# Values over 96 partitions with sums moved by small transfers, flat keys for the second batch, and another order up to the 4th chunk

## The chip, the cores and the metric

The kernel runs on one core of a Trainium2 chip. The time is that of one execution on the device in microseconds; it is taken three times, and the median counts. Besides, one execution was recorded by the profiler, and the rows below come from it.

## The reference

Pooled attention is followed by a gated product. Batch and heads are 8 and 8, the sequence is 576 and a head 64 wide; keys and values are averaged over groups of 8 positions, which leaves 72 keys for each head. The weights come as float64.

```
k_p = k.reshape(B, H, Sp, 8, D).mean(axis=3);  v_p = the same of v        # Sp = 72
attn = softmax(q @ k_p^T / sqrt(D));  x = (attn @ v_p) as (4608, 512)
a = x @ w1;  b = x @ w2                                                  # 512 x 1024 each
out = ((a * b) @ w3) @ w_out                                             # w3 1024 x 1024, w_out 1024 x 512
```

## The kernel before

The product `w3 @ w_out` is formed once on the chip (`W`, 8 tiles), so that a token chunk needs `x @ w1`, `x @ w2`, their product and one product with `W`. Each of these is made of three passes over a high and a low part of both factors (`PASSES`). The 4608 tokens are 12 chunks `m` of 384.

**The start** turns float64 into float32 by bit operations: a load brings 512 KB of raw words (`load_wo`, `load_w3`, `load_w12`), `w_high` takes the upper word on ScalarE (L140), `w_low` the rest of the fraction on VectorE (L145) or ScalarE (L150), `w_or` joins them on VectorE (L154). Tiles of `w3` are transposed by TensorE (`w_turn`, L183) and split (`t_hi`, `t_lo`), those of `w_out` split alone (`o_hi`, `o_lo`), and `w_mm s it` (L613, three passes of 128x512) adds them into `W`; there are 16 `s` with 4 `it` each. The same is done to the tiles of w1 and w2 (`w12_high`, `w12_low`, `w12_or`, `w12_hi`, `w12_lo`).

**A chunk** is, for each of 8 `j`: `a_mm` and `b_mm` (12 matmuls each, L538), `g_mul`, `g_hi`, `g_lo` and `out_mm` (9 matmuls, L582), which adds into three banks. The attention of chunk n + 1 lies between the matmuls of chunk n: `s_mm` (L415, scores), `soft_max` to `soft2`, a turn of the weights (`pt_mm` with `pt_post`, L475 and L485, in the first two chunks; `pt_turn` on VectorE and `pt_move` by DMA, L491 and L498, after them), `av_mm` (L512, 32 rows of keys at a time), and `x_hi`, `x_lo`.

**Keys and values** of a batch come in tiles of 2 x 8 x 64 floats a partition (`load_k`, `load_v`, four buffers `st`), and a tree of three additions on GpSimd (`pool_tree`, L373, L374, L378) sums the groups of 8. For the values each of three steps `r` reads 32 keys a head that overlap with the next step's, in four transfers of 32 partitions, and the sums are written into `vm` where `av_mm` reads them. Keys of a batch in `FLAT` come row by row over 128 partitions (three loads, the last a small one); of the others a load brings two heads over 72 partitions (four loads). `kt_mm` (L350) transposes the sums, and `kt_post` scales them into `kbd`.

**The order** of all steps is written out in `ORDER` up to some place in chunk 3; what isn't in it follows by the numbers of `at(...)`. Every engine takes its own instructions in that order, one after another, and waits for what it needs; a transfer that must wait on SyncE (SP) holds up all transfers behind it, and at most 8 transfers are on their way. Tables say which engine takes a step that two could take (`LOW_ACT`, `LOW_DVE`, `LO_DVE`, `O_POOL`, `K_DVE`, `Q_DVE`, `PT_DVE`, `A_DVE`). The cells of the raw words of w1 and w2 are those that earlier weight tiles leave: `load_w12 0 0` takes the cell of the first w_out tile, free after `w_mm 8` has run for all four `it`, `load_w12 7 1` that of `w_mm 15`.

Of the kernel before, what the change touches and what calls it, by code (L numbers as in the profile page):

```python
# [19 lines left out]
def kernel(  # L20
# [766 lines left out]
    for b in range(1, B):  # L787
# [13 lines left out]
        load_w3 2; w_high w3 2; w_or wo 0; o_hi 0; w_low w3 2; load_wo 2; w_or w3 2; w_turn 2; t_hi 0;
        w_mm 0 0 (0,); t_lo 0; w_mm 0 2 (0,); w_mm 0 3 (0,); warm 4; o_lo 0; w_mm 0 2 (1,); w_mm 0 0 (1,);
        w_mm 0 1 (0,); w_high wo 2; w_low wo 2; load_w3 1; w_mm 0 3 (1,); w_high w3 1; w_low w3 1;
        w_mm 0 3 (2,); load_w3 3; w_or w3 1; w_turn 1; w_mm 0 1 (2,); w_or wo 2; t_hi 2; w_mm 0 2 (2,); t_lo 2;
        o_hi 2; o_lo 2; w_mm 2 3 (0,1,2); load_wo 1; load_wo 3; w_high wo 1; w_low wo 1; w_or wo 1;
        w_mm 2 0 (0,1,2); load_w3 6; w_high w3 3; t_hi 1; w_low w3 3; o_hi 1; w_mm 2 2 (0,1,2); w_mm 1 3 (0,);
        w_low wo 3; t_lo 1; w_mm 0 1 (1,); w_mm 1 1 (0,); load_wo 4; w_high wo 3; load_w3 4; w_mm 1 1 (2,);
        o_lo 1; w_mm 1 2 (1,); load_w3 5; w_mm 1 3 (2,); w_mm 0 0 (2,); w_high w3 6; load_w3 7; load_wo 5;
# [145 lines left out]
```

## Time and profile before

| | us |
|---|---|
| median of three runs (lowest, highest) | 737.97 (737.64, 738.20) |
| the profiled execution | 739.05 |
| its span, first to last instruction | 737.2 |
| TensorE busy within the span | 722.3 |
| VectorE, ScalarE, GpSimd busy | 402.4, 228.6, 158.2 |

The profiled execution's own time is 1.85 us more than its span. TensorE is busy for 98% of the span; a matmul that waits at half speed counts as busy too, so that the idle time is read beside the granted clock.

### The profile page before, as it was taken

To read this page: it belongs to the slowest core of one execution; us is meant where nothing else is said; L and a number is where in the kernel's file an instruction comes from. 1 tells how busy PE (TensorE), PEld (TensorE's weight loads), DVE (VectorE), ACT (ScalarE), POOL (GpSimd) and SP (SyncE) were. 2 spreads that over 40 slices of the span, in tenths; PEclk is the share of its full clock that TensorE was granted. 3 is DMA by queue.
4 is the path that set the end of the run, shared out by engine and by line. 5 is a ranking of instruction groups with operands and counts; after the bars stand their busy time and mean duration, and the time that the engine had idled before them with its cause. 6 is when DMAs were issued, how large, how long until landed. Compare 5 with 4: busy or idle time off the path is not lost.

```text
span 737.2 us, 13685 instructions
## 1 busy us (share of the span) xinstructions
PE 722.3 (98%) x5466; PEld 652.9 (89%) x5466; DVE 402.4 (55%) x785; ACT 228.6 (31%) x506; POOL 158.2 (21%) x176
## 2 busy tenths in 40 slices
PE   6998999999999999999999999999999999999997
PEld 4876899998998999998998999998998999998997
DVE  6887976663653653743753742843743743732211
ACT  6886664222222222222222222222212222222211
POOL 1443438403305000025045100034054000000000
PEclk9999999999999999999999999999999999999999
DMA  9989962337240121153255130253345230210101
GB/s 332 354 263 242 239 175 60 57 97 157 59 131 12 61 68 25 64 125 85 78 131 123 65 79 9 73 129 72 101 116 114 82 70 2 82 27 1 43 1 44
DMA packets 124495, 74.57 MB, mean 101 GB/s; under 512 B 76176, under 2 KB 108176, under 8 KB 124432
## 3 DMA queue, kind: packets, MB, share of 16 engines
q1 hardware_dynamic: 124288, 73.57, 37.7%
q8 instruction: 43, 0.70, 0.4%
q14 instruction: 20, 0.16, 0.1%
q10 hardware_dynamic: 144, 0.13, 0.1%
HBM read 52.43 MB, written 9.44 MB: 84 GB/s over the span
## 4 chain that ended last, share of the span: by engine, by line
PE 92%; DMA 5%; SPq 1%; DVE 1%; issue 1%; POOL 0%; ACT 0%; DVEq 0%; POOLq 0%
PE o L582 26%; PE a L538 26%; PE b L538 26%; PE o L613 4%; PE a L512 3%; DMA raw<-in_moe_w_dram 2%; PE att L415 2%; DMA st<-in_k_dram 1%; PE att L183 1%; DMA PT<-T 1%; PE a L415 1%; PE a L613 1%; SPq L498 1%; PE att L512 1%; PE b L613 0%
## 5 line engine op out<-in xcount | busy, mean ns | idle before, releaser
L538 PE MATMUL a<-xT,hl 128*128 128x384 f32 x1152 | 217.5, 336 | 0.0
L538 PE MATMUL b<-xT,hl 128*128 128x384 f32 x1152 | 216.6, 335 | 0.0
L538 PEld LDWEIGHTS a<-xT,hl 128*128 128x128 f32 x1152 | 203.5, 188 | 6.9
L538 PEld LDWEIGHTS b<-xT,hl 128*128 128x128 f32 x1152 | 200.6, 188 | 1.1 <-issue 0.3
L582 PE MATMUL o<-Wc,gh 128*128 128x512 f32 (+1 forms) x576 | 180.4, 394 | 0.0
L556 DVE TENSOR_TENSOR a<-b,a 128x384 f32<-128x384 f32 x96 | 52.9, 552 | 196.3 <-PE b L538 190.5
L373 POOL TENSOR_TENSOR st<-st 128x512 f32<-128x512 f32 (+1 forms) x51 | 68.2, 1338 | 354.8 <-DMA st<-in_k_dram 262.7
L582 PEld LDWEIGHTS o<-Wc,gh 128*128 128x128 f32 x576 | 105.8, 189 | 23.0 <-issue 5.0
L582 PE MATMUL o<-Wc,gl 128*128 128x512 f32 (+1 forms) x288 | 113.2, 393 | 0.0
L561 ACT CAST gh<-a 128x384 fp32r<-128x384 f32 x96 | 49.3, 513 | 193.6 <-DVE a L556 181.8
L548 ACT COPY a<-a 128x384 f32<-128x384 f32 x92 | 44.1, 480 | 179.6 <-PE a L538 158.2
L567 DVE TENSOR_TENSOR gl<-a,gh 128x384 fp32r<-128x384 f32 x96 | 57.0, 595 | 29.2 <-ACT gh L561 29.2
L582 PEld LDWEIGHTS o<-Wc,gl 128*128 128x128 f32 x288 | 54.1, 188 | 12.2
L440 ACT ACTIVATE EB<-EB 128x288 f32<-128x288 f32 x66 | 29.4, 445 | 79.7 <-DVE EB L432 79.7
L491 DVE STREAM_TRANSPOSE T<-EB 128x768 f32<-128x768 f32 x30 | 46.8, 1561 | 10.9 <-DMA PT<-T 10.6
L452 DVE TENSOR_REDUCE sm<-EB 128x4 f32<-128x288 f32 x66 | 29.6, 450 | 25.8 <-ACT EB L440 25.8
L613 PE MATMUL o<-hl 128*128 128x512 f32 x144 | 40.3, 410 | 0.0
L374 POOL TENSOR_TENSOR st<-st 128x256 f32<-128x256 f32 (+1 forms) x51 | 38.9, 764 | 4.0
L613 PEld LDWEIGHTS o<-hl 128*128 128x128 f32 x144 | 26.6, 193 | 5.3 <-DVE Wc L624 0.2
L512 PE MATMUL a<-PT,vm 32*64 32x384 f32 (+1 forms) x192 | 28.1, 417 | 2.4 <-ACT PT L485 1.7
L459 DVE TENSOR_TENSOR EB<-EB,sm 128x576 f32<-128x576 f32 x36 | 28.3, 786 | 1.3
L512 PE MATMUL att<-PT,vm 32*64 32x384 f32 (+1 forms) x576 | 28.6, 419 | 0.3 <-DVE qT L301 0.3
(89 smaller groups left out, 560.3 us busy)
## 6 DMA issues: line engine op xcount, KB each, us to landing
raw<-in_moe_w_dram SPq DMA_DIRECT2D x32, 512.0 KB
st<-in_v_dram SPq DMA_DIRECT2D x96, 128.0 KB
PT<-T SPq DMA_DIRECT2D x120, 96.0 KB
out_dram<-ob SPq DMA_DIRECT2D x35, 256.0 KB
st<-in_k_dram SPq DMA_DIRECT2D x28, 288.0 KB
qs<-in_q_dram SPq DMA_DIRECT2D x112, 48.0 KB
raw<-in_moe_w_out_dram SPq DMA_DIRECT2D x8, 512.0 KB
qs<-in_q_dram SPq DMA_DIRECT2D x96, 24.0 KB
```

The source lines that it names most:

```text
L373: nc.gpsimd.tensor_tensor(out=t[:, :, 0:4], in0=t[:, :, 0:4], in1=t[:, :, 4:8], op=ALU.add)
L374: nc.gpsimd.tensor_tensor(out=t[:, :, 0:2], in0=t[:, :, 0:2], in1=t[:, :, 2:4], op=ALU.add)
L452: nc.vector.tensor_reduce(out=Mt[n, t][1][:, hs], in_=parts(Et[n, t])[:, hs], axis=AX.XY, op=ALU.add)
L491: nc.vector.transpose(out=T.rearrange("p g u i -> p u g i"), in_=Et[n, t][:, :NU * P].rearrange("p (u j g) -> p u g j", u=NU, g=4))
L512: nc.tensor.matmul(out=ps[g][D * c:D * c + D, off:off + cnt], lhsT=vm[b % 2][rows, r, c], rhs=PT[n][rows, cc, 2 * r + c], start=(r == 0), ...
L538: nc.tensor.matmul(out=o, lhsT=w12[j, w][sw][:, kt * P:(kt + 1) * P], rhs=x[sx][:, kt], start=(i == 0), stop=(i == 3 * NK - 1))
L548: (nc.vector.tensor_copy if (m, j) in A_DVE else nc.scalar.copy)(out=a, in_=stage.pop(("a", m, j))[:, :CH])
L556: nc.vector.tensor_tensor(out=g, in0=ps[:, :CH], in1=g, op=ALU.mult)
L561: nc.scalar.copy(out=gh, in_=g)
L567: nc.vector.tensor_tensor(out=gl, in0=g, in1=f(gh), op=ALU.subtract)
L582: nc.tensor.matmul(out=oacc[m][t][x][:, cols], lhsT=(gh, gl)[sg][:, c], rhs=W[j][sw][:, cols], start=(j == 0 and i == 0), stop=(j == NJ - ...
L613: nc.tensor.matmul(out=wacc[h][it], lhsT=w3t[s][sa][:, it * P:(it + 1) * P], rhs=wo[j][sb], start=n == 1, stop=n == 3 * NJ)
```

## The change

Four things change. Values: a step `r` now holds the keys 3k + r, so that its 24 keys a head don't overlap; one transfer brings them over 96 partitions (4 heads x 24 keys, twice), the tree writes the sums into a new tile `vp`, and `move_v` copies them into `vm` by 8 transfers of 24 partitions a batch, issued by SyncE. The scores' keys are put in the same order by `kt_post`, which reads with a step of three. Second: `FLAT` has batch 1 as well. Third: the tables name other engines. Fourth: `ORDER` is another one, up to the same stretch, and `out_mm` may come in any order of `j`.

```diff
-    EW = 2 * P + 4
+    EW = 2 * P
-    LO_DVE = [(1, 1), (3, 0), (3, 1), (5, 1), (6, 1)]
-    FLAT = (0,)
+    LO_DVE = [(1, 0), (3, 0), (4, 1), (5, 0), (7, 1)]
+    FLAT = (0, 1)
-    LOW_ACT = [6 of w3, 3 of wo]
+    LOW_ACT = [8 of w3, 7 of wo]
-    O_POOL = [0, 3, 4, 6]
+    O_POOL = [2, 4]
-    K_DVE = [(0, 2), (1, 0), (1, 2), (1, 3)]
+    K_DVE = [(1, 3)]
...
+        nc.gpsimd.memset(vm[i], 0.0)
...
     def load_v(b, r):
         t = stage["v", b, r] = st_tile([P, 2, POOL, D])
-        keys = v[b, :, KG * r * POOL:(KG * r + 32) * POOL].rearrange("(g c) (k e) d -> g k c (e d)", c=2, e=POOL)
-        for g in range(4):
-            nc.sync.dma_start(out=t[32 * g:32 * g + 32].rearrange("p c e d -> p c (e d)"), in_=keys[g])
+        rows = v[b].rearrange("h (k r e) d -> r (h k) (e d)", r=KS, e=POOL)[r]
+        nc.sync.dma_start(
+            out=t[:VP].rearrange("p s e d -> p s (e d)"), in_=rows.rearrange("(s p) x -> p s x", p=VP))
...
     def prep_v(b, r):
-        pool_tree(stage.pop(("v", b, r)), vm[b % 2][:, r])
+        if b not in vp:
+            vp[b] = p1.tile([P, 2, KS, D], F32, tag="vp", name="vp")
+        pool_tree(stage.pop(("v", b, r))[:VP], vp[b][:VP, :, r])
+
+    def move_v(b, s):
+        for i in range(4):
+            g, c = divmod(4 * s + i, 2)
+            nc.sync.dma_start(out=vm[b % 2][32 * g:32 * g + KW, c], in_=vp[b][KW * i:KW * i + KW, s])
...
     def out_mm(m, j):
-        if j == 0:
+        if m not in oacc:
...
+        for s in range(2):
+            at("L", prep[-1] + 2, move_v, b, s)
...
     ORDER = """
-        load_wo 0; w_high wo 0; warm 5; w_low wo 0; load_w3 0; w_high w3 0; w_low w3 0; w_or w3 0; w_turn 0;
+        warm 5; load_w3 0; w_low w3 0; w_high w3 0; load_wo 2; w_high wo 2; w_or w3 0; warm 3; warm 4; w_turn 0;
```

The first place is SyncE's queue at the program's start (`raw` from `moe_w` is a tile of w3, from `moe_w_out` one of w_out). Before:

```order
L120 DMA raw<-in_moe_w_out_dram 128x1024
L125 DMA raw<-in_moe_w_dram 128x4x256 x2
L120 DMA raw<-in_moe_w_out_dram 128x1024
L125 DMA raw<-in_moe_w_dram 128x4x256 x2
L120 DMA raw<-in_moe_w_out_dram 128x1024 x2
```

And in the change:

```order
L126 DMA raw<-in_moe_w_dram 128x4x256
L121 DMA raw<-in_moe_w_out_dram 128x1024 x2
L126 DMA raw<-in_moe_w_dram 128x4x256
L121 DMA raw<-in_moe_w_out_dram 128x1024
L126 DMA raw<-in_moe_w_dram 128x4x256 x2
```

The tile of the second `w_turn` (`load_w3 2`) was the third transfer and is the fourth now; that of the first `w_turn` was the second and is the first.

The second place is SyncE's queue from the transfers behind the last w3 tile to the last keys of batch 1 (`raw` are tiles of w1 and w2 here, `qs` queries of chunk 1, `st` values with L370, keys with L322). Before:

```order
L370 DMA st<-in_v_dram 32x2x512 x4
L131 DMA raw<-in_moe_w_dram 128x4x256 x2
L286 DMA qs<-in_q_dram 64x6x64 x4
L322 DMA st<-in_k_dram 72x2x512
L370 DMA st<-in_v_dram 32x2x512 x4
L131 DMA raw<-in_moe_w_dram 128x4x256
L322 DMA st<-in_k_dram 72x2x512
L131 DMA raw<-in_moe_w_dram 128x4x256 x3
L286 DMA qs<-in_q_dram 64x6x64 x2
L131 DMA raw<-in_moe_w_dram 128x4x256
L322 DMA st<-in_k_dram 72x2x512
```

And in the change, from `load_w12 0 0` on (the rows with L395 are `move_v 0 0` and `move_v 0 1`):

```order
L132 DMA raw<-in_moe_w_dram 128x4x256 x2
L373 DMA st<-in_v_dram 96x2x512
L323 DMA st<-in_k_dram 64x512
L287 DMA qs<-in_q_dram 64x6x64 x4
L132 DMA raw<-in_moe_w_dram 128x4x256
L287 DMA qs<-in_q_dram 64x6x64 x2
L132 DMA raw<-in_moe_w_dram 128x4x256 x2
L287 DMA qs<-in_q_dram 64x6x64 x2
L395 DMA vm_84<-vp 24x192 x4
L323 DMA st<-in_k_dram 128x2x512 x2
L395 DMA vm_84<-vp 24x192 x4
L132 DMA raw<-in_moe_w_dram 128x4x256 x6
```

All keys of batch 1 now stand in front of the third w1 tile, and the second half of the moves stands behind two key loads of 512 KB.

The third place is ScalarE's queue up to the last copy of `PT` ahead of the first `av_mm` (`wb<-raw` are `w12_high` and `w12_low`, `hl<-att` is `t_hi`, `hl<-wb` is `w12_hi`, `PT` is `pt_post`). Before:

```order
L150 ACTIVATE wb<-raw 128x512
L233 CAST hl<-wb 128x512
L188 CAST hl<-att 128x512
L485 COPY PT<-a 128x2x4x32
L140 ACTIVATE wb<-raw 128x512
L150 ACTIVATE wb<-raw 128x512
L485 COPY PT<-a 128x2x4x32
L140 ACTIVATE wb<-raw 128x512
L620 CAST Wc<-o_469 128x512
L485 COPY PT<-att 128x4x4x32
```

And in the change:

```order
L151 ACTIVATE wb<-raw 128x512
L189 CAST hl<-att 128x512
L234 CAST hl<-wb 128x512
L499 COPY PT<-a 128x2x4x32
L234 CAST hl<-wb 128x512
L499 COPY PT<-att 128x4x4x32
L141 ACTIVATE wb<-raw 128x512
L499 COPY PT<-att 128x4x4x32
```

Before, a `w12_low` (of w2's second tile) stands between the `PT` copies; now the last `w12_low` ahead of them is that of `load_w12 1 0`, and one `w12_high` of the same tile stands between the last two copies.

## Rows read from the trace of the kernel before

**Rows 1.** The page: busy time, share of the span and instructions of each engine

```profile
PE 722.3 (98%) x5466; PEld 652.9 (89%) x5466; DVE 402.4 (55%) x785; ACT 228.6 (31%) x506; POOL 158.2 (21%) x176
```

**Rows 2.** Stretches: busy of PE, PEld, DVE, ACT, POOL; granted clock, DMA share, GB/s

```profile
0.00:20.00 20.00, 12.99 (x57) 10.38 (x57) 12.42 (x23) 13.08 (x22) 4.77 (x10) 1.00 0.94 336
60.00:80.00 20.00, 18.00 (x124) 13.22 (x122) 15.93 (x21) 11.94 (x24) 7.67 (x6) 0.91 1.06 249
```

**Rows 3.** Waits of TensorE: total us, times, longest

```profile
PE att L183 <- DVE Wc L154: 5.7, 2, 4.9
PE a L512 <- ACT PT L485: 1.7, 1, 1.7
PE att L350 <- POOL km L378: 1.5, 1, 1.5
```

**Rows 4.** Timeline of ScalarE, first 10 us: start, us, instruction, idle before

```profile
5.93 0.67 ACT L140 ACTIVATE Wc<-raw 128x512 f32<-128x512 f32 x1 [0.90 <-DMA raw<-in_moe_w_dram]
7.78 0.68 ACT L140 ACTIVATE Wc<-raw 128x512 f32<-128x512 f32 x1 [1.18 <-DMA raw<-in_moe_w_dram]
...
9.34 0.69 ACT L140 ACTIVATE wt<-raw 128x512 f32<-128x512 f32 x1
```

**Rows 5.** Chain that ended last, to 51 us: start, us, what

```profile
10.35 0.85 PE o L613 x2
...
12.91 0.49 PE a L613 x2
...
48.10 3.46 PE o L613 x15
```

**Rows 6.** Timeline of TensorE at the first `av_mm` and the first `a_mm`

```profile
68.57 0.50 PE L512 MATMUL a<-PT,vm 32*64 32x384 f32 x1 [1.73 <-ACT PT L485]
...
76.57 2.27 PE L538 MATMUL a<-xT,hl 128*128 128x384 f32 x12
```

**Rows 7.** Timeline of ScalarE, 55 to 68 us

```profile
55.61 0.32 ACT L446 ACTIVATE EB<-att,mx 128x72 f32<-128x72 f32 x1 [0.30 <-DVE mx L427]
...
57.99 0.71 ACT L150 ACTIVATE wb<-raw 128x512 int32<-128x512 uint16 x1
...
65.98 0.67 ACT L150 ACTIVATE wb<-raw 128x512 int32<-128x512 uint16 x1 [3.60 <-DMA raw<-in_moe_w_dram]
66.55 0.35 ACT L485 COPY PT<-a 128x256 f32<-128x256 f32 x1
66.81 0.66 ACT L140 ACTIVATE wb<-raw 128x512 f32<-128x512 f32 x1
...
67.83 0.60 ACT L485 COPY PT<-att 128x512 f32<-128x512 f32 x1
```

**Rows 8.** Chain that ended last, three of its pieces

```profile
72.57 10.11 DMA st<-in_k_dram
...
86.11 0.41 PE att L350 x3
...
161.79 2.33 DMA PT<-T
```

**Rows 9.** Stretches of 5 us, columns as in rows 2

```profile
25.00:30.00 5.00, 5.00 (x25) 4.15 (x23) 4.39 (x8) 4.78 (x9) 1.30 (x1) 1.00 1.11 342
...
50.00:55.00 5.00, 5.00 (x56) 3.97 (x55) 3.62 (x6) 4.67 (x10) 2.71 (x4) 1.00 0.96 287
55.00:60.00 5.00, 5.00 (x25) 4.10 (x24) 4.76 (x13) 4.51 (x21) 0.45 (x1) 1.00 1.05 208
60.00:65.00 5.00, 5.00 (x32) 4.25 (x30) 4.03 (x5) 2.38 (x5) 3.31 (x3) 1.00 1.10 236
...
70.00:75.00 5.00, 5.00 (x48) 2.59 (x49) 4.87 (x6) 3.41 (x9) 2.60 (x1) 0.66 1.05 222
```

**Rows 10.** Timeline of TensorE at the third chunk's `av_mm`, and what follows it

```profile
170.45 0.50 PE L512 MATMUL a<-PT,vm 32*64 32x384 f32 x1 [0.65 <-DMA PT<-T]
...
172.57 0.73 PE L582 MATMUL o<-Wc,gh 128*128 128x512 f32 x2
```

More of the change, by code (lines that the diff above doesn't have):

```diff
@@ L85 @@
     kbd = [cp.tile([P, NPR, KP], F32, name=f"kbd{i}") for i in range(2)]
-    vm = [cp.tile([P, KS, 2, D], F32, name=f"vm{i}") for i in range(2)]
+    vm = [cp.tile([P, 2, KS, D], F32, name=f"vm{i}") for i in range(2)]
     EB = [cp.tile([P, KS * EW], F32, name=f"EB{i}") for i in range(2)]
@@ L575, in out_mm @@
         g, gh, gl = gt.pop((m, j))
+        k = stage["out", m] = stage.get(("out", m), 0) + 1
         for t in range(3):
@@ L799 @@
     ORDER = """
-        load_wo 0; w_high wo 0; warm 5; w_low wo 0; load_w3 0; w_high w3 0; w_low w3 0; w_or w3 0; w_turn 0;
[L801 to L808, printed above, removed]
-        w_mm 1 0 (0,); w_or w3 3; w_turn 3; w_mm 1 3 (1,); w_or wo 3; o_hi 3; w_mm 2 1 (0,1,2); w_low w3 6;
@@ new lines @@
+        pt_mm 0 1 4 6; pt_post 0 2 4 6; w12_low 1 0; w12_lo 0 0; t_hi 15; t_lo 15; w12_hi 0 1; w12_lo 0 1;
+        pt_post 0 1 4 6; w_mm 14 2 (0,1,2); prep_k 1 0; w_mm 15 2 (0,1,2); prep_k 1 1; pt_mm 0 1 0 4;
+        w12_hi 1 1; q3_post 1 0; move_v 0 1; pt_post 0 2 0 4; q3_turn 1 1; w12_high 1 0; q3_post 1 1;
+        w_mm 14 3 (0,1,2); w12_or 1 0; w12_lo 1 1; load_w12 2 0; pt_post 0 1 0 4; av_mm 0; w12_hi 1 0;
+        w12_low 2 0; x_hi 0 0; w_mm 15 1 (0,1,2); w_mm 15 0 (0,1,2); w_hi 1 1; w_mm 15 3 (0,1,2);
@@ new lines @@
+        w_mm 14 0 (0,1,2); x_hi 0 1; x_lo 0 0; x_lo 0 1; q3_turn 1 3; x_hi 0 2; x_lo 0 2; x_hi 0 3; x_lo 0 3;
+        load_w12 3 0; w_hi 1 0; w_lo 1 0; warm 1; w_hi 1 2; q3_post 1 3; a_mm 0 0; w12_low 2 1; load_w12 7 1;
+        w_hi 1 3; w_lo 1 3; w12_lo 1 0; q3_turn 1 2; q3_post 1 2; prep_k 1 2; a_post 0 0; w12_high 2 0;
+        w12_high 3 0; load_w12 3 1; w12_high 2 1; b_mm 0 0; s_mm 1 (0,); w12_low 3 0; w12_or 2 1; load_w12 4 1;
+        w12_or 2 0; w12_hi 2 0; w12_high 3 1; w12_hi 2 1; a_mm 0 1; g_mul 0 0; soft_max 1 0 0 0; kt_mm 1;
@@ new lines @@
+        load_w12 6 1; w12_low 5 1; w12_high 6 1; w12_or 6 0; w12_lo 5 0; w12_or 5 1; w12_hi 5 1;
+        soft_max 1 2 0 0; pt_mm 1 0 0 4; w12_low 6 1; w12_lo 4 1; w12_hi 6 0; g_mul 0 3; g_hi 0 3;
+        soft_max 1 2 1 0; b_mm 0 4; pt_post 1 0 4 6; w12_lo 5 1; prep_v 1 1; prep_v 1 2; load_k 2 2;
+        soft_sub 1 2 0 0; soft_exp 1 2 0; w12_lo 6 0; a_mm 0 5; b_mm 0 5; g_mul 0 4; g_hi 0 4; g_lo 0 4;
+        a_post 0 5; g_lo 0 3; out_mm 0 3; soft_sub 1 2 1 0; soft_sum 1 2 0; move_v 1 1; soft_exp 1 2 1;
@@ new lines @@
+        pt_mm 1 1 4 6; soft_sum 1 2 1; w12_high 7 1; w12_high 7 0; out_mm 0 4; g_mul 0 5; soft2 1 2; g_hi 0 5;
+        w12_low 7 1; w12_or 7 1; pt_post 1 1 4 6; move_v 1 0; tr_q 2 0; w12_or 6 1; load_k 2 0; w12_hi 6 1;
+        w12_hi 7 1; pt_mm 1 1 0 4; pt_mm 1 2 4 6; w12_low 7 0; pt_post 1 1 0 4; pt_post 1 0 0 4; w12_lo 6 1;
+        pt_post 1 2 4 6; pt_mm 1 2 0 4; pt_post 1 2 0 4; w12_lo 7 1; a_mm 0 6; a_post 0 6; w12_or 7 0; tr_q 2 2;
+        load_k 2 1; tr_q 2 3; w12_hi 7 0; w12_lo 7 0; load_k 2 3; b_mm 0 6; g_mul 0 6; av_mm 1; g_lo 0 5;
@@ L913 @@
+        prep_v 3 2; move_v 3 0; move_v 3 1
     """
```

222 lines of the change are left out of this document (107 added, 115 removed).

## The prediction

> **What bounds the kernel now.** I read the page first: TensorE is busy for 722.3 of 737.2 us [rows 1], so the span is TensorE's work plus its holes, and the change takes next to nothing out of that work. What can be won are the holes and the stretches at half speed. The stretches show where they are: 12.99 busy in the first 20 us, 18.00 in 60 to 80 at a mean clock of 0.91 [rows 2]. TensorE's waits name them [rows 3]: 5.7 us for the first tiles of w3, 1.7 at an `av_mm` for a `PT` copy, 1.5 at `kt_mm` for the sums of the keys. The stretches behind about 180 us are dense in this trace, and the two orders agree there, so all that follows lies in the first 180 us.
>
> *The start.* ScalarE's timeline shows the first w3 tile landed at 5.93, the third transfer at 7.78, the fourth before 9.34 [rows 4]. The first `w_mm` runs at 10.35, two passes in 0.85, 0.43 each; the pair at 12.91 takes 0.49, and later fifteen take 3.46, 0.23 each [rows 5]. So 10.35 to about 12.9 runs at half speed.
>
> *The first `av_mm`.* TensorE arrives at 68.57 − 1.73 = 66.84 and waits for ScalarE's `PT` copy [rows 6]. ScalarE's timeline says why: it stood 3.60 us at 65.98, at the `w12_low` of a tile of w2 whose load had not landed, and the copies stand behind it in its queue [rows 7]. The price is more than 1.73: in 70 to 75 the granted clock is 0.66 [rows 9], a mix of both levels. From 68.57 to the first `a_mm` at 76.57, 8.00 us, TensorE did one `av_mm` and twelve passes. The third chunk's `av_mm` at full clock takes 172.57 − 170.45 = 2.12 [rows 10], and twelve passes 2.76, together 4.88. The other 3.1 is what half speed cost.
>
> *The keys of batch 1.* The chain goes back to a key load issued at 72.57 that lands 10.11 later, then GpSimd's tree, then `kt_mm` at 86.11 [rows 8]; TensorE waited 1.49 there (1.5 in the waits).
>
> **The change part by part.**
>
> *Start: +1.5.* The second turn needs `load_w3 2`, now the fourth transfer, and no `w_mm` may run ahead of it in TensorE's queue. Third and fourth transfer lie at most 9.34 − 7.78 = 1.56 apart. The first tile comes one transfer earlier (that gains nothing, since the second turn decides). Half speed after the start may last longer with the later begin: nothing to 1.2 us more; I take 0.6.
>
> *Work ahead of the first `av_mm`: 0.* By the order both versions run the same there, 180 passes of `w_mm`, sixteen turns of w3, six of queries, the same transposes. TensorE would arrive at 66.84 + 1.5 + 0.6 = 68.9.
>
> *ScalarE ahead of it: no wait.* Between `kt_mm 0` and `av_mm 0` TensorE now has 69 passes (15.9), 46 transposes (a turn of a tile is four; by 0.41 for three [rows 8] less than 0.14 each, I take 0.11: 5.1) and three score tiles (2.0 by estimate), 23.0 in all, 22.3 behind `kt_mm` itself. ScalarE has in the same piece 4 scalings, 15 conversions, 7 casts, 16 exponentials, 2 products and 4 `PT` copies. From the starts in its timeline [rows 7]: eight exponentials 57.99 − 55.61 = 2.38, a conversion 66.55 − 65.98 = 0.57, a conversion with a cast 67.83 − 66.81 = 1.02, so a cast 0.45, a copy up to 0.60. That is 8.6 + 3.2 + 4.8 + some 3.7 for the rest, 20.3, and 68.57 − 67.83 = 0.74 from the last copy to the matmul: 21.0. ScalarE is ready about 1 us early if no load holds it; the `w12_low` that stood 3.60 is behind the copies now. VectorE gives up work to it, GpSimd takes some: neither bounds this stretch.
>
> *Values and `move_v`: the new wait.* `av_mm` now needs the second half of the moves, which SyncE issues behind two 512 KB key loads, and all transfers ahead of them count. The count goes from `load_w12 0 0`, which must wait for `w_mm 8` on all four `it`. In the old order that place is within the fifteen passes at 48.10 [rows 5], at 48.8; in the new one six passes, a turn and a score tile less are ahead of it (2.5), and 2.1 is added by the start: 48.4. From there on 5 tiles of weights (2.62 MB), a value load (0.39), three key loads (1.18), eight query loads (0.79) and the moves (0.15) are 5.13 MB. The stretch of the same kind, 50 to 55, moves 287 GB/s [rows 9]: 17.9 us. A small transfer takes 2.33 from issue to landing [rows 8], so the last move lands at 68.6, against 68.9: no stall, but hardly any slack. The bounds: 342 GB/s, as in 25 to 30 where only loads over 128 partitions run [rows 9], gives 65.7; 208, as in 55 to 60 [rows 9], gives 75.4. I take 287: the low rows hold loads of 32 and of 72 partitions, of which none is left in this stretch.
>
> The Trainium skill, "SBUF — State Buffer", section "Door 1: The DMA port swizzle", says that a transfer's bandwidth goes by how many of the 16 ports its partitions reach; by its table 32 partitions at the start reach eight, 96 reach all. By that rule the new value load is as fast as a full one, and the row for 25 to 30 is the one to take: the move lands at 65.7 and the stall is out of reach. The row of 208 GB/s agrees in direction, but it mixes both narrow forms with full loads.
>
> *Gains.* If `av_mm` starts at 68.9 without a wait, the wait of 1.73 is paid by the start's 2.1: +0.4 at that place. The clock is then not lost behind it: −3.1. The two full key loads of batch 1 stand ahead of the third w1 tile instead of behind it, so by the sum above they land before 69, and three additions on GpSimd end some 10 us ahead of `kt_mm 1`: −1.49. If that cover were gone, the 1.49 is back.
>
> *Losses.* Flat keys need six transposes instead of four: +0.3. Small waits at the new places of conversions, TensorE's queue against ScalarE's and VectorE's: nothing to 1.5, I take 0.4.
>
> *At nothing:* clearing of `vm` on GpSimd at the start, which has 4.77 us of work in the first 20 [rows 2]; the scaling's strided read (0.3 at most a time, under the passes); moves of later batches (8 issues a batch on SyncE behind loads that land many chunks ahead; uncovered, each batch would cost up to 2.33); `out_mm` in another order of `j`, the same matmuls. The 0.65 wait at the third `av_mm` [rows 10] for the weights' transfer I leave.
>
> **Sum.** +0.4 − 3.1 − 1.5 + 0.3 + 0.4 = −3.5. The profiled execution took 739.05, so 735.55; the median of the runs is 737.97, a factor of 0.9985: **734.5**. Terms by their bounds (start +1.3 to +2.8, clock 2.8 to 3.2, small waits 0 to 1.5) give 733.2 to 736.3 for this case. Less than 0.2%, 1.5 us, is about what a measurement of this kernel can't tell from no change.
>
> **The rivals.**
>
> *The moves land late.* With a stall of s at `av_mm` the clock falls as it did after 1.73 (a wait of 0.65 did not lower it [rows 10]), so 3.1 isn't won: 0.4 + s − 1.49 + 0.7 = s − 0.4. Slower by over 1.5 from s = 1.9 on, a landing after 70.8, which is a mean rate under 255 GB/s. The row 60 to 80 has 249 [rows 2]: landing 71.3, s = 2.4, +2.0, about 740.0. At 208, s = 6.5, +6.1, 744. For it: rows of 208, 236 and 222 [rows 9] in this neighbourhood, and that a value load or a move waiting for GpSimd holds up the queue behind it. Against: those stretches hold the transfers that the change removes. With s between 1 and 1.9 it comes out the same, 738.6 to 739.4.
>
> *The clock is kept, but the wait only moves:* ScalarE's slack of 1 us is used up by loads that land late at its 15 conversions, or the cold start is longer, so that 2 to 3 us of the gain go in waits between 14 and 66 or behind 77, where the old order shows none. About 737, no difference that can be told.
>
> *Only keys count:* `av_mm` waits for another thing of about 1.7 (a conversion ahead of the copies, the value tree), the clock falls as before, and the start's 1.5 cancels the 1.49 of the keys: 738.
>
> **How the numbers follow.** My forecast 0.55; moves late 0.23 (0.16 slower, 0.07 same); moved waits or only keys 0.22 (0.15 same, 0.04 slower, 0.03 faster). Faster 0.57, same 0.23, slower 0.20 (0.54 and 0.01 of the forecast's 0.55 go to faster and same). The range reaches from just under the forecast's own bounds over the same cases to the late moves at 249 GB/s; about 0.1 is left above it and 0.08 below: 733.0 to 740.2.
>
> **What the profile of the changed kernel would show.** First `w_mm` at about 11.9 (at 10.6 or earlier the start's term is wrong). The first `av_mm` starts near 68.9 with no releaser, or a wait under 0.7; if the moves are late, the releaser is a transfer `vm<-vp`, and the sum is wrong. The granted clock in 70 to 75 is 1.00, and the first `a_mm` comes at about 73.7 instead of 76.57. No wait at `kt_mm 1`; a wait there for GpSimd puts the key loads wrong. Rates in 48 to 66 between 287 and 342 GB/s. From the third chunk on, TensorE's work runs a constant 3.5 us ahead of the old trace. A ScalarE that waits for `raw` between 50 and 66 would make the second rival right.

## The result, and the profile after

The changed kernel is slower: 747.52 us median (745.19 to 748.69, four executions) against 737.81 for the kernel before (734.54 to 738.20, four executions), a ratio of 1.0138 with an interval of 1.0098 to 1.0177. The prediction of 734.5, range 733.0 to 740.2, is wrong in sign. The profiled execution took 748.36 us, 9.31 more than that of the kernel before.

The page's first part, and from its fourth part the shares of the chain that ended last, of the changed kernel:

```profile
PE 727.2 (97%) x5468; PEld 654.8 (88%) x5468; DVE 397.1 (53%) x775; ACT 232.5 (31%) x516; POOL 160.4 (21%) x185
...
PE 68%; DMA 11%; SPq 8%; DVE 6%; issue 3%; ACT 2%; POOL 1%; DVEq 0%; POOLq 0%
```

The same shares in the kernel before:

```profile
PE 92%; DMA 5%; SPq 1%; DVE 1%; issue 1%; POOL 0%; ACT 0%; DVEq 0%; POOLq 0%
```

TensorE has 4.9 us more busy time than in [rows 1], which is hardly more work (two instructions more): a matmul that waits for its operands can count as busy, as in the product at 395.69 below. The chain says more. Before, it runs through TensorE for 92% of the span; after, for 68%, and SyncE's own issuing (`SPq`) has 8% of it where it had 1%. Releasers are inferred, so the shares are a direction and no measure.

Where the time goes is read from the attention's products, which come once a chunk in both kernels. The timeline of TensorE in the kernel before at the `av_mm` of the 5th and of the 12th chunk:

```profile
281.99 0.37 PE L512 MATMUL a<-PT,vm 32*64 32x192 f32 x1
...
664.05 0.53 PE L512 MATMUL a<-PT,vm 32*64 32x384 f32 x1
```

And in the changed kernel, with the places that the prediction named (first `w_mm`, waits ahead of the first `av_mm`, that `av_mm` and what follows it, first `a_mm`, a later wait), the same two `av_mm` last:

```profile
11.68 1.63 PE L628 MATMUL o<-hl 128*128 128x512 f32 x3
...
57.20 1.36 PE L628 MATMUL o<-hl 128*128 128x512 f32 x3 [0.84 <-ACT hl L189]
...
67.19 0.44 PE L489 MATMUL a<-ident,EB 128*128 128x128 f32 x2 [1.21 <-DVE EB L473]
...
72.46 0.53 PE L526 MATMUL a<-PT,vm 32*64 32x384 f32 x1
...
73.78 0.81 PE L526 MATMUL att<-PT,vm 32*64 32x384 f32 x2 [0.46 <-DMA vm<-vp]
...
76.31 0.97 PE L628 MATMUL o<-hl 128*128 128x512 f32 x3
...
79.44 2.36 PE L552 MATMUL a<-xT,hl 128*128 128x384 f32 x12
...
111.08 2.34 PE L552 MATMUL b<-xT,hl 128*128 128x384 f32 x12 [1.59 <-DVE a L570]
...
286.54 0.37 PE L526 MATMUL a<-PT,vm 32*64 32x192 f32 x1
...
673.52 0.53 PE L526 MATMUL a<-PT,vm 32*64 32x384 f32 x1
```

Up to the 5th chunk the change has lost 286.54 − 281.99 = 4.6 us. From the 5th to the 12th `av_mm` it takes 386.98 instead of 382.06, another 4.9. So there are two losses of about the same size, and the second lies where the prediction had put nothing. Of the first, 2.9 are there at the first `a_mm` (79.44 − 76.57), the rest comes behind it.

**The first `av_mm`.** It starts at 72.46, 3.9 later than in [rows 6], and lasts to 76.31, 3.85 where a product at full clock takes 2.12 [rows 10], because the second half of its moves lands only when the product has begun. The transfers that SyncE issues ahead of it, in its timeline (start of the first, time for all, how many):

```profile
48.55 0.99 SPq L132 DMA_DIRECT2D raw<-in_moe_w_dram  x2
...
50.74 4.36 SPq L287 DMA_DIRECT2D qs<-in_q_dram  x4
55.49 1.84 SPq L132 DMA_DIRECT2D raw<-in_moe_w_dram  x1
58.11 2.12 SPq L287 DMA_DIRECT2D qs<-in_q_dram  x2
60.47 0.98 SPq L132 DMA_DIRECT2D raw<-in_moe_w_dram  x2
61.50 2.15 SPq L287 DMA_DIRECT2D qs<-in_q_dram  x2
63.75 4.06 SPq L395 DMA_DIRECT2D vm<-vp  x4
67.87 1.01 SPq L323 DMA_DIRECT2D st<-in_k_dram  x2
68.93 3.44 SPq L395 DMA_DIRECT2D vm<-vp  x4
```

The stretches of 5 us over the same time, columns as in rows 2:

```profile
45.00:50.00 5.00, 4.76 (x53) 3.56 (x51) 3.45 (x5) 4.53 (x17) 2.21 (x4) 1.00 1.07 265
50.00:55.00 5.00, 5.00 (x55) 3.98 (x54) 3.87 (x9) 1.82 (x9) 4.10 (x5) 1.00 1.10 311
55.00:60.00 5.00, 4.02 (x48) 2.52 (x46) 2.77 (x6) 4.55 (x10) 0.34 (x1) 1.00 1.20 184
60.00:65.00 5.00, 5.00 (x27) 4.10 (x27) 4.97 (x8) 4.79 (x21) 3.72 (x4) 1.00 1.02 275
65.00:70.00 5.00, 3.79 (x23) 2.92 (x22) 4.68 (x10) 3.56 (x9) 0.32 (x1) 1.00 0.48 87
70.00:75.00 5.00, 4.54 (x44) 3.09 (x50) 2.44 (x3) 2.77 (x6) 3.75 (x4) 1.00 0.85 293
```

The reader is to see the second column of SyncE's rows beside the last two of the stretches. Eight query loads take SyncE 4.36 + 2.12 + 2.15 = 8.63 us, the eight moves 4.06 + 3.44 = 7.50. Of the 23.8 us from 48.55 to the end of the last move's issue, 72.37, the rows that stand here have 20.95 of issuing. From 45 to 65 the DMA engines are full (shares of 1.02 to 1.20) and move 184 to 311 GB/s, so that some of the issue time there may be waiting for them. In 65 to 70, where about half of the moves are issued, they are busy for 0.48 and move 87: there they wait for SyncE. GpSimd's last value tree ends at 62.63 (its load, issued at 49.63, is there only at 59.66), so the moves could not have begun more than 1.1 us earlier. The chain's row for the second half of the moves:

```profile
68.93 4.72 DMA vm<-vp
```

It lands at 73.65, and TensorE goes on at 73.78.

**ScalarE and VectorE.** ScalarE's timeline at the raw load that it waits for:

```profile
55.45 0.68 ACT L151 ACTIVATE wb<-raw 128x512 int32<-128x512 uint16 x1 [3.63 <-DMA raw<-in_moe_w_dram]
```

This is `w12_low 0 0`; behind it in the queue stand `t_hi 13`, for which TensorE waits 0.84 at 57.20, and the copies. The wait of 3.60 in [rows 7] was not removed, another load has it now.

VectorE is late as well. Two of its `w_or`, and two a little later:

```profile
61.08 3.35 DVE L155 SCALAR_TENSOR_TENSOR Wc<-Wc 128x512 int32<-128x512 int32 x2
...
67.66 1.28 DVE L155 SCALAR_TENSOR_TENSOR wb<-wb 128x512 int32<-128x512 int32 x2
```

The first two take 3.35 us while GpSimd works on the last value tree and a split of weights (59.66 to 63.88), the later two 1.28 while GpSimd is idle. The `EB` for which TensorE waits 1.21 at 67.19 stands behind the first two in VectorE's queue. That GpSimd's work is what makes them long was not tried.

**The later products.** SyncE, GpSimd and TensorE of the changed kernel around the `av_mm` at 395.69, a fence for each:

```profile
384.63 5.25 SPq L267 DMA_DIRECT2D qs<-in_q_dram  x8
389.97 6.22 SPq L395 DMA_DIRECT2D vm<-vp  x8
```

```profile
377.37 0.46 POOL L382 TENSOR_TENSOR vp<-st 96x128 f32<-96x128 f32 x1
```

```profile
395.69 0.53 PE L526 MATMUL a<-PT,vm 32*64 32x384 f32 x1
...
396.73 0.50 PE L526 MATMUL att<-PT,vm 32*64 32x384 f32 x1 [0.17 <-DMA vm<-vp]
...
399.48 0.73 PE L597 MATMUL o<-Wc,gh 128*128 128x512 f32 x2
```

GpSimd has the sums ready at 377.83. The moves stand behind key loads and eight query loads in SyncE's queue, begin 12 us later, and take 0.78 each to issue. The product lasts 3.79 instead of 2.12. TensorE's waits name only 0.17 of that; the rest shows only in the product's length, so waits alone would have hidden it. The product at 562.05 lasts 3.47 in the same way: +1.67 and +1.35.

The number of issues did not grow. Between the 5th and the 12th product SyncE issues 297 transfers in the kernel before and 293 in the changed one, 152.6 and 158.2 us added up from the traces: 48 value loads (0.43 us of SyncE each, median) have become 12, and 32 moves (0.71 each) are new. What differs is where they stand. SyncE of the kernel before has eight of its value loads around the same place, behind 24 query loads:

```profile
393.31 3.67 SPq L370 DMA_DIRECT2D st<-in_v_dram  x8
```

### The profile page after: what moved, and what is told of

Read it like the earlier page. It is cut to its first block, busy times and chain, and to the rows that moved or that the text cites. A ratio compares the mean times of both kernels' runs of the same rounds, so it can differ in the third digit from the quotient of the medians.

```text
span 746.6 us, 13634 instructions
## 1 busy us (share of the span) xinstructions
PE 727.2 (97%) x5468; PEld 654.8 (88%) x5468; DVE 397.1 (53%) x775; ACT 232.5 (31%) x516; POOL 160.4 (21%) x185
## 4 chain that ended last, share of the span: by engine, by line
PE 68%; DMA 11%; SPq 8%; DVE 6%; issue 3%; ACT 2%; POOL 1%; DVEq 0%; POOLq 0%
PE o L597 20%; PE b L552 20%; PE a L552 20%; DMA raw<-in_moe_w_dram 5%; SPq L267 3%; PE a L526 2%; DMA st<-in_k_dram 2%; SPq L395 2%; SPq L512 1%; DMA st<-in_v_dram 1%; PE o L628 1%; PE att L429 1%; DVE EB L446 1%; DVE T L505 1%; DMA PT<-T 1%
## 5 line engine op out<-in xcount | busy, mean ns | idle before, releaser
L377 POOL TENSOR_TENSOR st<-st 96x512 f32<-96x512 f32 (+3 forms) x54 | 71.2, 1319 | 353.8 <-DMA st<-in_k_dram 241.3
L581 DVE TENSOR_TENSOR gl<-a,gh 128x384 fp32r<-128x384 f32 x96 | 60.3, 630 | 36.0 <-ACT gh L575 35.9
L628 PE MATMUL o<-hl 128*128 128x512 f32 x144 | 42.5, 419 | 1.0 <-ACT hl L189 0.8
L378 POOL TENSOR_TENSOR st<-st 96x256 f32<-96x256 f32 (+3 forms) x54 | 42.2, 782 | 4.2
L526 PE MATMUL att<-PT,vm 32*64 32x384 f32 (+1 forms) x576 | 30.5, 409 | 0.6 <-DMA vm<-vp 0.6
L278 DVE STREAM_TRANSPOSE qT<-qs 128x384 f32<-128x384 f32 x40 | 22.1, 564 | 15.9 <-DMA qs<-in_q_dram 15.9
```

The lines of the kernel that those rows point to most:

```text
L377: nc.gpsimd.tensor_tensor(out=t[:, :, 0:4], in0=t[:, :, 0:4], in1=t[:, :, 4:8], op=ALU.add)
L378: nc.gpsimd.tensor_tensor(out=t[:, :, 0:2], in0=t[:, :, 0:2], in1=t[:, :, 2:4], op=ALU.add)
L526: nc.tensor.matmul(out=ps[g][D * c:D * c + D, off:off + cnt], lhsT=vm[b % 2][rows, c, r], rhs=PT[n][rows, cc, 2 * r + c], start=(r == 0), ...
L581: nc.vector.tensor_tensor(out=gl, in0=g, in1=f(gh), op=ALU.subtract)
L628: nc.tensor.matmul(out=wacc[h][it], lhsT=w3t[s][sa][:, it * P:(it + 1) * P], rhs=wo[j][sb], start=n == 1, stop=n == 3 * NJ)
```

## The experiments

"Early" is the start of the 5th chunk's `av_mm` (281.99 in the first profile of the kernel before, 281.30 in the second), "late" the time from there to the 12th chunk's (382.06 and 382.07), both from TensorE's timeline. Ratios are to the kernel before on the same chip. "Early" is of one execution each and scatters: e1 and the changed kernel are the same up to there and lie 1.3 apart, e6 and e12 are one kernel and lie 5.2 apart. The profiled execution of e13, 749.44, was the slowest of its four.

| kernel | median us | ratio [95%] | early | late |
|---|---|---|---|---|
| changed kernel | 747.52 | 1.0138 [1.0098, 1.0177] | 286.54 | 386.98 |
| e1 moves one step earlier | 744.12 | 1.0097 [1.0076, 1.0117] | 285.27 | 384.45 |
| e2 raw load's work behind the copies | 747.97 | 1.0144 [1.0122, 1.0166] | 286.99 | 386.14 |
| e3 moves together | 747.40 | 1.0145 [1.0124, 1.0166] | 287.75 | 386.17 |
| e4 both | 747.74 | 1.0147 [1.0125, 1.0168] | 286.30 | 385.83 |
| e5 moves on GpSimd | 752.62 | 1.0221 [1.0199, 1.0242] | 295.58 | 382.14 |
| e6 old values, new order | 747.61 | 1.0140 [1.0116, 1.0164] | 285.70 | 382.31 |
| e12 the same kernel, one execution | 747.84 | – | 290.85 | 382.10 |
| e7 before, raw loads' work behind | 736.91 | 1.0008 [0.9991, 1.0026] | 279.95 | 382.04 |
| e8 e7, keys earlier | 737.16 | 1.0008 [0.9993, 1.0024] | 280.46 | 382.08 |
| e11 before, one execution | 738.21 | – | 281.30 | 382.07 |
| e9 e1 + e2 + e3, one more step moved | 743.18 | 1.0090 [1.0074, 1.0107] | 285.78 | 382.56 |
| e10 e9, first transfers as before | 743.84 | 1.0097 [1.0080, 1.0114] | 284.47 | 384.88 |
| e13 e1, two weight loads ahead of queries | 747.55 | 1.0141 [1.0118, 1.0164] | 291.40 | 383.20 |
| e14 e9, the same two loads | 745.86 | 1.0125 [1.0105, 1.0145] | 287.88 | 384.42 |
| e15 e14, moves on GpSimd | 746.54 | 1.0122 [1.0102, 1.0143] | 289.86 | 382.17 |

**e1_move_step: the moves of the later batches one step earlier in `plan_v`.**

```diff
-            at("L", prep[-1] + 2, move_v, b, s)
+            at("L", prep[-1] + 1, move_v, b, s)
```

> The changed kernel with the moves of batches 2 and up one place earlier in the plan (at the step behind the last tree of the values, not two steps behind it), so that on SyncE they stand ahead of the eight query loads. First theory (the moves come too late because they stand in SyncE's queue behind loads, long after the sums are there): the two long first-chunk products of batches 4 and 6 (3.79 and 3.47 us instead of 2.12) go back to 2.1, the time falls by about 3.0 us, to 744.5, and nothing changes in the first 180 us. Rival (the later part is slower because sums come later over 96 partitions, or by queries that land late): no change, 747.5, or the wait goes to the query loads that are now behind the moves.

The edit reaches the moves of batches 4 to 7 alone, since `ORDER` places those of batches 0 to 3. The median is 3.4 lower, with both long products back at 2.12; 2.5 of that lie in the late part, the rest is scatter ahead of it. The intervals of the two ratios just overlap; that of e1 and those of e2, e3 and e4, which were timed together, do not. SyncE's timeline at the same place, and the wait that is new in TensorE's list:

```profile
382.86 6.60 SPq L395 DMA_DIRECT2D vm<-vp  x8
...
390.09 3.75 SPq L267 DMA_DIRECT2D qs<-in_q_dram  x8
```

```profile
PE a L429 <- DVE qT L278: 1.8, 2, 1.0
```

Moves and queries have changed places, and now two score steps wait for their queries, up to 1.0 each. Late is still 2.4 longer than before the change. That rest is not fixed: e9, e10, e13 and e14 have the same order behind the 5th product and lose 0.5, 2.8, 1.1 and 2.4 there.

**e2_w12_behind, e3_move_first, e4_both: the two waits at the first `av_mm`, each alone and together.** e2 puts the work on the raw load behind the copies, e3 the second half of the moves behind the first, ahead of the key loads.

```diff
-  w12_low 0 0; soft_sub 0 1 1 0; w12_high 0 0; pt_mm 0 0 0 4; w_or w3 12; w12_or 0 0; t_hi 13;
+  soft_sub 0 1 1 0; pt_mm 0 0 0 4; w_or w3 12; t_hi 13;
...
-  t_lo 12; load_q3 1 2;
+  t_lo 12; w12_low 0 0; w12_high 0 0; w12_or 0 0; load_q3 1 2;
```

```diff
-  move_v 0 0; load_k 1 0;
+  move_v 0 0; move_v 0 1; load_k 1 0;
...
-  q3_post 1 0; move_v 0 1;
+  q3_post 1 0;
```

> The changed kernel with ScalarE's two conversions of the first w1 tile, and VectorE's joining of them, put behind the work of the tiles of w3 that stood behind them. Theory (ScalarE's wait of 3.63 us for that tile's load holds up the turns and the copies of PT, and with them TensorE): TensorE's waits at 57 and 67 us shrink by 2 to 3 us together. Since the value moves land at 74.2 by SyncE's queue, the time itself falls by 0.5 to 2.5 us, to 745 to 747. Rival (the moves alone set the first av_mm): TensorE waits as much longer at the av_mm, no change, 747.5.

> The changed kernel with the second half of the moves of batch 0 right behind the first half, ahead of the two 512 KB key loads. Theory (the second half lands behind these loads): the last move lands near 71 instead of 74.2, the first av_mm takes 2.1 to 2.5 instead of 3.85, and the time falls by 1.5 us, to 746. The keys land some 3 us later and their sums are still in time for kt_mm 1 at 87. Rival (ScalarE's copies set the start, and the first av_mm waits for nothing else): 747.5.

> e2 and e3 together. If ScalarE's wait and the moves each hold up the first av_mm in turn, together they give more than their sum alone: first av_mm at 69 to 70, the first a_mm at about 75 to 76 instead of 79.4, the time 743.5. If only one of them counts, the time is that of the better of e2 and e3. If neither, 747.5.

None of the three is faster. With e3 and e4 the first product does last 2.2 and begins at 71.1 to 71.2, 1.3 earlier, but the gain is gone at the next step. VectorE and TensorE of e4 behind that product:

```profile
76.68 1.22 DVE L146 TENSOR_SCALAR wb<-raw 128x512 int32<-128x512 int32 x1 [4.88 <-DMA raw<-in_moe_w_dram]
```

```profile
78.89 0.78 PE L296 MATMUL att<-ident,qs 128*128 128x128 f32 x3 [2.44 <-DVE xT L537]
79.32 3.77 PE L552 MATMUL a<-xT,hl 128*128 128x384 f32 x12
```

`w12_low 2 0` waits 4.88 for its load, with the split of x behind it in VectorE's queue. TensorE waits 2.44, and its next twelve passes take 3.77 instead of 2.36: half speed follows the wait (the mean granted clock is 0.995 to 0.998 in all ten executions of e3 and e4). `a_mm` is at 79.32, against 79.44. One wait hid the next.

**e5_moves_pool: the moves issued by GpSimd.**

```diff
-            nc.sync.dma_start(out=vm[b % 2][32 * g:32 * g + KW, c], in_=vp[b][KW * i:KW * i + KW, s])
+            nc.gpsimd.dma_start(out=vm[b % 2][32 * g:32 * g + KW, c], in_=vp[b][KW * i:KW * i + KW, s])
```

> The changed kernel with all value moves issued by GpSimd instead of SyncE, at the same places of the order. Theory (eight moves cost SyncE 6.1 us of issuing for each batch; put earlier in its queue, as in the run before, they free the product but make the queries behind them late, which is what was left there: one wait of about 1 us before the scores of each of two chunks): the time from the second chunk on is that of the old kernel again, the whole falls by some 4.9 us to 742.6 (against 744.1 with the earlier place). Rival (what is left in the later part is not SyncE's): 744 or more. The first 75 us may change by 1 us either way, since the loads behind the moves are issued earlier.

Slower at the start, since the second half of batch 0's moves stands behind two key trees in GpSimd's queue (issued from 78.70 on). TensorE's list:

```profile
PE att L526 <- DMA vm<-vp: 5.9, 1, 5.9
```

But late is 382.14, that of the kernel before: with the issuing off SyncE the second loss is gone.

**e6_old_values and e12_old_values_again, one kernel profiled twice: the new order with the values of before.**

```diff
-        for s in range(2):
-            at("L", prep[-1] + 2, move_v, b, s)
...
-  move_v 0 0; load_k 1 0;
+  load_k 1 0;
```

with `load_v`, `prep_v`, `kt_post` and `vm` as in the kernel before.

> The changed kernel with the values as in the old one (four transfers of 32 partitions a step, sums written where they are read, no moves), all else as changed. Theory (the later part's loss comes from the moves alone): the later part falls back by 4.9 us; the part up to the first a_mm stays late by ScalarE's wait for the first w1 tile and the slower start, and by 32-partition loads: 741 to 743. Rival (the new order loses there without the moves): above 745. Second rival (the moves also cause the whole loss ahead of the first a_mm): 738 or less.

> The run with the old values in the new order once more, for its trace: its profiled execution took 742.9, five others 746.5 to 748.6. If this trace is of the slower kind, the difference of some 4.7 us shows as one or two waits of TensorE between 60 and 130 us that are longer or are followed by half speed. If it is again 743, the difference stays open.

Late is back (382.31, 382.10), but the median is not lower: the rival of the expectation, a loss in the new order without the moves, is what came. TensorE's timeline and the stretch behind it, first of e6, then of e12:

```profile
110.68 2.32 PE L538 MATMUL b<-xT,hl 128*128 128x384 f32 x12 [3.15 <-ACT hl L233]
```

```profile
115.00:120.00 5.00, 5.00 (x27) 4.44 (x26) 4.46 (x9) 3.00 (x6) 3.19 (x4) 1.00 0.41 118
```

```profile
113.38 4.18 PE L538 MATMUL b<-xT,hl 128*128 128x384 f32 x12 [3.35 <-ACT hl L233]
```

```profile
110.00:115.00 5.00, 1.65 (x6) 1.66 (x6) 3.29 (x7) 3.25 (x7) 2.08 (x2) 0.73 0.27 70
115.00:120.00 5.00, 5.00 (x19) 5.00 (x19) 1.83 (x4) 0.51 (x1) 4.69 (x7) 0.59 0.17 62
```

The change without its values (new order, tables and flat keys of batch 1) costs a wait of over 3 us at that `b_mm` for a weight tile, with no move in the program. Nearly the same wait of the same kernel is followed by full speed in one execution (742.90) and by half speed in the other (747.84). The other five timed runs of e6 lie at 746.5 to 748.6, near the second, with a mean granted clock of 0.993 to 0.998 against 1.000 in the first.

**e7_old_behind, e8_old_behind_keys, e11_old_again: the kernel before with its `av_mm` wait taken away, and as it is.** In e7 the conversions on which the copies waited stand behind them; e8 also brings the keys of batch 1 forward. They try the prediction's two gains without the change's costs.

```diff
-  w12_high 0 1; q3_turn 1 0; w12_low 1 1;
+  w12_high 0 1; q3_turn 1 0;
...
-  q3_post 1 1; prep_k 1 3;
+  q3_post 1 1; w12_low 1 1; w12_high 1 1; w12_or 1 1; w12_hi 1 1; prep_k 1 3;
...
-  av_mm 0; w12_low 2 0; w12_low 2 1; w12_high 2 1; x_hi 0 0;
+  av_mm 0; x_hi 0 0;
...
-  x_lo 0 2; a_mm 0 0;
+  x_lo 0 2; w12_low 2 0; w12_low 2 1; w12_high 2 1; w12_or 2 1; a_mm 0 0;
```

> The old kernel, all as it was but for the order of w1's and w2's conversions around the first av_mm: those of w2's second tile stand behind the last PT copy and the query copies, those of the third tiles behind x_lo. Theory (the prediction's reading of the old trace: ScalarE's wait of 3.60 us for a load costs 1.73 at the av_mm and 3.1 of half speed behind it): the first a_mm at about 72 instead of 76.6; but the keys of batch 1 land as late as before, so kt_mm 1 waits 4 to 6 us instead of 1.5, and the whole gains 0 to 1.5 us: 735.6 to 737. Rival (the wait is only shifted to VectorE's x_lo or to a value tree): first a_mm at 75 or later, 737.

> The run before with the last two key loads of batch 1 ahead of four query loads and three weight loads. Theory: the keys land near 74 instead of 82.7, kt_mm 1 doesn't wait, and both gains stand: 4.8 and 1.5, 731 us, faster than both kernels. Rival (the weight loads pushed back make an a_mm or b_mm wait, or the first a_mm isn't earlier): 735 to 737.

> The old kernel once more, for its trace. If the half speed behind the first av_mm belongs to the kernel, this trace has the granted clock near 0.66 in 70 to 75 again and its own time is near 739. If it belongs to that one execution, the clock is 1.0 there, and the time is at 736 to 737; then 3.1 of the prediction's 3.5 us were not there to be won in most executions.

Neither is faster: 736.91 and 737.16, both 1.0008 with intervals across 1. In e7 `av_mm` starts at 67.7 with no wait and lasts 2.2, but `a_mm` at 74.11 then waits 1.18 for `xT`. In e8 `kt_mm 1` does not wait any more, but TensorE waits 1.58 for a query load at 78.87 instead. The second profile of the kernel before tells why there was less to win than [rows 9] say. Its stretch and its TensorE:

```profile
70.00:75.00 5.00, 4.73 (x55) 2.54 (x56) 4.89 (x6) 4.11 (x9) 2.63 (x1) 1.00 0.99 273
```

```profile
69.92 0.50 PE L512 MATMUL a<-PT,vm 32*64 32x384 f32 x1 [0.88 <-ACT PT L485]
...
76.29 1.92 PE L538 MATMUL a<-xT,hl 128*128 128x384 f32 x10
```

A wait of 0.88 instead of 1.73, full clock behind it, and `a_mm` at 76.29 against 76.57. The half speed that the prediction meant to win belonged to one execution: the mean granted clock is 0.997 in the first profiled execution, and 0.999 or 1.000 in 50 of the 52 executions of this kernel timed beside the experiments. The time of this second profile, 738.21, is still not the 736 to 737 that was expected with full clock.

**e9_chain and e10_chain_start: all known waits of the start at once.** e9 is e1, e2 and e3 with `w12_low 2 0` behind the split of x, e10 also has the first w3 tiles as first and third transfer.

```diff
-  av_mm 0; w12_hi 1 0; w12_low 2 0; x_hi 0 0;
+  av_mm 0; w12_hi 1 0; x_hi 0 0;
...
-  x_hi 0 3; x_lo 0 3;
+  x_hi 0 3; x_lo 0 3; w12_low 2 0;
```

> The changed kernel with every wait that the runs so far showed one behind the other taken away together: the first w1 tile's conversions behind the w3 tiles' (as in e2), the second half of the moves ahead of the key loads (e3), VectorE's conversion of the third w1 tile, at which it stood 4.88 us in e4, behind x_lo, and the later moves one place earlier (e1). Theory (a chain of waits for loads, each hidden by the next): the first a_mm at 76 to 77 instead of 79.4, full clock there, 3 us, and 3.4 us from the later moves: 741. Rival (the next conversion or load takes over again): 744, the time of e1 alone.

> e9 with the old kernel's kind of start: the w_out tile that the first product needs is the second transfer and the second turn's w3 tile the third again. Theory (the prediction's start term of 1.5 us, and all that follows is moved with it): the first w_mm at 10.3 instead of 11.9, 1.5 us less than e9. Rival (behind 45 us the loads set the pace, and an earlier start of TensorE only makes it wait longer there): no difference from e9.

e9 is the best of the changed order: 743.18, `a_mm` at 77.70, late 382.56. Its late part loses only 0.5 with all moves still on SyncE. A wait of 1.68 at 110.42 stays. In e10 the second turn comes at 9.92 instead of 11.34, the first `w_mm` only at 11.76 instead of 12.11 (it waits 0.72 for ScalarE), `a_mm` at 76.54, and the 5th product 1.3 earlier than in e9; but 2.3 are lost in the late part, where TensorE's list has 2.2 for queries, and the median is not lower. Whether an earlier start carries through is not settled by it.

**e13_only_loads, e14_chain_loads, e15_chain_loads_pool: the weights of 111 us.** In the changed kernel `load_w12 5 1` and `6 1` are issued (at 102.03) behind sixteen query loads, of which SyncE's timeline shows the first eight:

```profile
83.28 10.54 SPq L267 DMA_DIRECT2D qs<-in_q_dram  x8
...
102.03 1.00 SPq L132 DMA_DIRECT2D raw<-in_moe_w_dram  x2
```

So I moved these two loads ahead of the queries: in e1 (e13), in e9 (e14), and in e9 with the moves on GpSimd right behind the values' tree (e15).

```diff
+  load_w12 5 1; load_w12 6 1; load_q 2 (0,);
-  load_q 2 (0,);
...
-  w12_hi 4 1; load_w12 5 1; a_post 0 4; w12_high 5 1; load_w12 6 1;
+  w12_hi 4 1; a_post 0 4; w12_high 5 1;
```

> e1 with the last two loads of w2 (for b_mm 0 5 and 0 6) ahead of the sixteen query loads of the third chunk, behind which SyncE issues them at 102 us. Theory (ScalarE waits 2.60 us for that load at 107, and TensorE 0.7 to 1.6 behind it at 110): these waits vanish, 1.5 to 2 us less than e1's 744.1: 742.4. Rival (the queries, 1 us later each, or the part ahead of 80 us set the pace): 744.

> e9 with the same two loads moved. Theory: e9's wait of 1.7 us at 110 goes, 741.4 instead of 743.2. Rival: 743.

> e14 with the moves issued by GpSimd, all eight right behind the value tree. Theory (SyncE's 6.1 us of issuing for each batch makes the queries late and is all that is left in the later part): the later part falls by 2 to 2.5 us more, 739, near the old kernel. Rival: 741 as e14, or more if GpSimd's issuing (4 us for eight moves) holds up its key trees or the splitting of weights.

This theory fell: 747.55, 745.86 and 746.54, slower than e1 and e9 by 3.4 and 2.7, and e15 no better. SyncE and ScalarE of e13:

```profile
81.83 6.86 SPq L132 DMA_DIRECT2D raw<-in_moe_w_dram  x4
```

```profile
105.63 0.66 ACT L141 ACTIVATE wb<-raw 128x512 f32<-128x512 f32 x1 [5.56 <-DMA raw<-in_moe_w_dram]
```

Now SyncE stands 6.86 us at four weight loads, queries and the next tile (`load_w12 6 0`) come later, and ScalarE waits 5.56 for that one. e15 confirms the other half: late 382.17 with SyncE free of moves.

## Why the prediction was wrong

*What held.* The first `w_mm` came at 11.68 (11.9 was predicted), `load_w12 0 0` is issued at 48.55 (48.4), `kt_mm 1` no longer waits, and the clock in 70 to 75 is 1.00. The rival "moves land late" names the right place and sign, and the sign by which "the wait only moves" was to be known, ScalarE waiting for `raw` between 50 and 66, is there as well, with 3.63. I gave them 0.23 and 0.22 (the latter with "only keys count") as alternatives; they came together, and neither had the later loss in its price.

*"5.13 MB … at 287 GB/s: 17.9 us".* This step failed. The last move landed at 73.65 instead of 68.6, between the bounds of 65.7 and 75.4, and the product lasted 1.73 longer for it. Three things are wrong in it. It began with an empty queue at `load_w12 0 0`, but in 45 to 50 the engines are full (1.07), in part with older loads. It took 287 GB/s, and the three stretches from 50 to 65 have 311, 184 and 275, a mean of 257. And it priced the moves by their bytes, 0.15 MB or 0.5 us; they took SyncE 7.50, with the engines half idle behind it. From the end of the value tree alone, 62.63, eight issues of 0.72 and the 1.28 from the last issue's end to landing give 69.7, an estimate from these rows; by it 68.6 was out of reach. A rate over bytes from a stretch of large loads can't price a stretch of small ones; the count of issues has to be taken beside it. By the rule that the prediction cites from the Trainium skill, "SBUF — State Buffer", section "Door 1: The DMA port swizzle", the moves would have landed at 65.7. By the same section's table 64 partitions from 0 or from 64 on reach eight ports, as 32 do, so the eight query loads are narrow too, which the prediction left out. The 184 GB/s of 55 to 60, the lowest row while the engines were full, came with query loads and without any load over 32 or 72 partitions; it agrees in direction, but the query loads also come in pieces of 256 bytes, and no run parts the two.

*"Moves of later batches: at nothing".* This is the larger single mistake, 4.9 us. The cover named was that the loads land many chunks ahead. But the moves wait for GpSimd's sums, not for the loads, and those are ready 18 us ahead of the product (377.83 to 395.69); between stand a query burst of 5.25 and the moves' own 6.22. The price per batch that the prediction gave for the uncovered case, up to 2.33, holds for the two long products (1.67 and 1.35); 0.7 is a score step that waits for queries, and about 1.2 I could not put to a place. That the moves on SyncE cause the loss is shown by four kernels: e1 moves it from the products to the queries, e5 and e15 take the issues from SyncE and have 382.14 and 382.17, and e6 has no moves and 382.31. It is their place and what they wait for, not the time of SyncE as such: e6 has SyncE issue 48 value loads in that part and loses nothing, and e9, with the moves at the earlier place on SyncE, loses 0.5. Why e1, e10 and e14 lose over 2 with the same order there stays open.

The Trainium skill, "DMA: Bandwidth & Descriptors", section "Issuing engines are not separate DMA queues", says that starting transfers from several engines saves only the sequencer's time to initiate them, "which is usually small relative to the DMA itself". The runs agree with the first half, as the late part of e5 and e15 shows. The second half does not fit these moves: one of 24 x 192 floats takes 0.78 of SyncE's time at 390, and in e5, issued by GpSimd, 1.7 from issue to landing (median).

*"ScalarE is ready about 1 us early if no load holds it".* The condition decided, and I had given it no landing time. A load held it for 3.63. "VectorE … neither bounds this stretch" failed too, by the 1.21 at 67.19. So TensorE came to the `av_mm` at 72.46, not at 68.9, and 2.05 of these 3.6 are its waits at 57.20 and 67.19.

*"The clock is then not lost: −3.1".* This was taken from one execution, and mis-sized in it: a clock of 0.66 over 5 us takes at most 1.7. The second profile of the kernel before has the wait of 0.88 with full clock and still needs 6.37 from `av_mm` to `a_mm` (76.29 − 69.92), so that half speed cost about 1.6 of the 8.00 and not 3.1. And e7, which removes the wait, gains nothing in the median. The gain expected was not there to be won in most executions. The keys' −1.5 was real at its place, but there is a new wait of 1.59 at 111.08 and, in e6, of 3.15.

*What stays open.* The early loss of about 4.6 has several parts that I can name (start, ScalarE's raw load, VectorE's `EB` at 67.19, the moves, the weights at 111) but can't add up: taking one away (e2, e3, e4, e13) let the next load's lateness through. e6 and e12 lose 3.7 and 8.9 early without any move, by the rest of the change; the tables and the flat keys of batch 1 were not tried alone. That the order of SyncE's queue up to 105 us as a whole sets it is argued from these shifts; no run put all the loads back in the old order with the rest of the change.

## What to carry to other kernels

When a step becomes transfers that wait for a computed result, look where they stand on their queue, how long one takes there, and what stands behind them: eight moves of 18 KB cost 6 us of SyncE, and the product or the queries behind them pay. The number of issues does not tell it: a batch had twelve value loads before and has three, with eight moves, now. The Trainium skill, "DMA: Bandwidth & Descriptors", section "Rules for kernel authors", advises to coalesce small transfers; no run here tries it for the moves. A wait in a profile is worth its size only when the next thing behind it is early; look what is due next on each engine before putting the wait's whole length, or a stretch of half speed that one execution shows, into a sum.

## What the runs showed of the hardware

A short wait of TensorE is not always followed by half speed: the same `b_mm` of the same kernel (e6, e12), after 3.15 and 3.35 idle, ran on at a granted clock of 1.00 in one execution and at 0.73 and 0.59 in the two stretches of the other, with 4.18 instead of 2.32 for its twelve passes. The length of the wait alone does not decide it: at 1.73 idle the clock fell in the first profile of the kernel before. The Trainium skill, "TensorE: Matmul & The Clock Gate", section "What's actually happening", says of the ramp at a kernel's start that it differs from run to run of one kernel; here a difference of that kind is seen in the middle of one. And eight query loads of 48 KB (L267) took SyncE 10.54 us at 83 in the changed kernel, where sixteen of the same size take 8.30 at 441; eight of 24 KB take 5.25 at 384, and 3.75 in e1 at 390. The first stand behind seven large loads issued in the 4.5 us before; how much of the 10.54 is waiting for room was not tried.
